# First loads over two queues, two transposes in a row, and z read back from DRAM, in a gated linear-attention kernel

## The chip, the cores and the metric

The kernel runs on one core of one Trainium2 chip. The metric is the device time of one execution in microseconds (us), the median of several runs. Beside it stands one execution that the hardware profiler recorded; all single durations below are from that one.

## What is computed

The function is a mixture of two blocks over the same x (2048 x 640, bf16), g * A(x) + (1 - g) * B, with its gradients to all inputs but B_x. A is linear attention with 32 heads of 20 columns, B a dense layer with ReLU. What matters here is the start of A, where keys are summed to z:

```
g = sigmoid((x * gate_w).sum(-1))
qkv = x @ wqkv                      # q, k, v: 32 heads of 20
pq, pk = phi(q), phi(k)             # phi(t) = t + 1 where t > 0, else exp(t), + 1e-6
kv  = einsum("bhsd,bhse->bhde", pk, v)
z   = einsum("bhsd->bhd", pk)       # sum of pk over the 2048 rows: 640 numbers
num = einsum("bhqd,bhde->bhqe", pq, kv)
den = einsum("bhqd,bhd->bhq", pq, z) + 1e-6
a   = (num / den) @ wo
b   = relu(x @ w1) @ w2
out = g * a + (1 - g) * b           # and the gradients of out
```

## The kernel before

x is cut into 16 chunks of 128 rows. The program goes through these stages, each a loop over chunks or over the five blocks of 128 columns:

1. First loads (lines 408 to 432). x chunks 0 to 4 come in as they are (`x_load`, L402, through `load_N`, L334); the other chunks are also loaded transposed by DMA (`load_T`, L325). wk is loaded in five blocks (`wk_load`, L405). SyncE (SP) and ScalarE (ACT) each issue DMAs from a queue of their own; instructions on one engine keep their order, and a DMA that has to wait holds what its engine has behind it.
2. The k phase (L477 to L507). `warm_up` (L459) runs matmuls on zeros. `xt(i)` (L437) transposes chunk i on TensorE (PE) and copies the result out of PSUM (L451, L452, or L347 by `copy_out`); chunks 3 and 4 share one PSUM tile of two banks, named xtp2 in the code and xtp_194 in the profile. `k_part(i, ks)` (L463) multiplies chunk i with blocks ks of wk; the tile is kp. After the last block come an exponential on ACT and two operations of VectorE (DVE), L396 and L397, which give pk. The PE order of chunks 0 to 4 is written out by hand (L478 to L502). The gate weights are transposed into an extra column of wk (L483, L484), so that k_part gives the gate too. The DMA transposes start after k_part(1, [2]) (L494).
3. `q_main(0)` and `q_main(1)` (L518), then the Y phase (L626 to L635): for each of five blocks m, Y = pk^T x over all chunks, with a column of ones behind x, so that column 640 of the PSUM tile yp is z for the block. ACT copies Y0 (L630), DVE the z column into `zc_t` (L633), 128 partitions by 5; DVE makes a diagonal block of it in `zd` (L634); SP transposes Y0 by DMA (L635).
4. z to all partitions (L637 to L639): ones times zd on PE gives z in every row (zp), ACT copies it to `zb`.
5. `h_half(i, half)` (L560): x @ w1, half a chunk's row; ReLU by ACT (L569, L572) or DVE (L574). `blockdiag` (L374): 50 small matmuls into bd, ACT copy (L385), ten DVE masks (L388), which give KVT. `q_den(i)` (L526) multiplies pq by zb on GpSimd (POOL, L528); `q_post(i)` (L530) reduces that on DVE (L534), takes the reciprocal, scales on POOL (L542) and transposes by DMA. `mt_tile(t)` (L647) needs KVT. `out_chunk(i)` (L587) needs the transposed h, the transposed pq and M.
6. The loop over pairs of chunks (from L671), and then the gradients, up to the last stage, which ends near 636 us.

The order of instructions on each engine is made by the framework's scheduler from the program's order and from its estimate of what is ready; only PE's order in stage 2 is fixed. PSUM tiles of tag PP share four buffers. The large SBUF buffers lie in one arena; the planner (`_Arena.plan`, L31) looks for an arrangement by seeded random reordering of the list of entries, with start and end times written by hand (L121 to L188), `zd` among them (L136).

The last gradient is stored near the end, from 128 partitions with five numbers each:

```
gcol = cpool.tile([P, KD], BF16, name="gcol")                          # L297
nc.scalar.dma_start(out_6.rearrange("(k p) -> p k", p=P), gcol[:])     # L1021
```

Of the kernel before, what the change touches and what calls it, by code (L numbers as in the profile page):

```python
# [8 lines left out]
ALU = mybir.AluOpType  # L9
AX = mybir.AxisListType  # L10
FP32 = mybir.dt.float32
BF16 = mybir.dt.bfloat16
PSUM = bass.MemoryType.PSUM

P = 128
# [66 lines left out]
def kernel(  # L82
# [5 lines left out]
    nc = tc.nc  # L88
    x2 = A_x.rearrange("b s d -> (b s) d")
# [3 lines left out]
    S, D = x2.shape  # L93
    F = B_w1.shape[1]
    NT = S // P
    KD = D // P
# [16 lines left out]
    ar = _Arena()  # L113
    B2 = 2
# [6 lines left out]
    T_Y, T_FF, T_DW2, T_X, T_FB, T_DW1, T_DWK, T_DX, T_END = 26, 48, 190, 273, 296, 432, 512, 556, 640  # L121
# [11 lines left out]
    ar.add("w1", KD * F * B2, 8, T_H)  # L133
    ar.add("w2", KF * D * B2, 12, T_DW2 + 10)
    ar.add("pk", NT * D * B2, 0, T_FF)
    ar.add("zd", D * B2, 0, T_FF - 5)  # L136
    ar.add("YT0", KD * D * B2, T_Y, T_FF + 5)
    ar.add("dzs", D * B2, T_X, T_FB + 50)
    ar.add("warm", 512 * B2, 0, 10)
# [55 lines left out]
    def aview(name, n_elems, **dims):  # L195
        o = ar.off(name) // 2
        v = arena[:, o:o + n_elems]
        if dims:
            (k, n), = dims.items()
            v = v.rearrange(f"p ({k} z) -> p {k} z", **{k: n})  # L200
        return v
# [7 lines left out]
    def mat(name):  # L209
        return aview(name, KD * D, k=KD)  # L210

    xN = aview("xN", NT * DQX, i=NT)
# [13 lines left out]
    xSg = [aview(f"xS{g}", G * D, k=KD) for g in range(NG)]  # L226
    doTg = [aview(f"doT{g}", G * D, k=KD) for g in range(NG)]
    hsg = [aview(f"hs{g}", G * FPAD, i=G) for g in range(NG)]
    zd, YT0_s = aview("zd", D), mat("YT0")
    dzs = aview("dzs", D)  # L230
    wk_s, wq_s, wv_s, wo_s = aview("wk", KD * DQX, k=KD), mat("wq"), mat("wv"), mat("wo")
    w1_s = aview("w1", KD * F, k=KD)
# [30 lines left out]

    dram = ctx.enter_context(tc.tile_pool(name="dram", bufs=1, space=bass.MemoryType.DRAM))
    pk_d = dram.tile([S, D], BF16, name="pk_d")
    pqg_d = dram.tile([S, D], BF16, name="pqg_d")
    KVT_d = dram.tile([D, D], BF16, name="KVT_d")
    e_d = dram.tile([S, D], BF16, name="e_d")
# [8 lines left out]
    cpool = ctx.enter_context(tc.tile_pool(name="const", bufs=1))  # L277
    tsb = ctx.enter_context(tc.tile_pool(name="ts", bufs=2))
    psp = ctx.enter_context(tc.tile_pool(name="ps", bufs=1, space=PSUM))
    ident = cpool.tile([P, P], BF16, name="ident")  # L280
# [2 lines left out]
                            pattern=[[-1, P]], channel_multiplier=1)  # L283
    gwb = cpool.tile([P, D], BF16, name="gwb")
    ones_sq = cpool.tile([P, P], BF16, name="ones_sq")
    zc_t = cpool.tile([P, KD], FP32, name="zc_t")
    MDw = cpool.tile([P, KD, BWID], BF16, name="MDw")
    zb = cpool.tile([P, D], BF16, name="zb")
    dzb = cpool.tile([P, D], BF16, name="dzb")
# [12 lines left out]
    def _nm(pfx):  # L302
        _cnt[0] += 1
        return f"{pfx}{_cnt[0]}"

    def pp(name="pp"):
        return psp.tile([P, 2, 512], FP32, tag="PP", bufs=4, name=_nm(name))
# [4 lines left out]
    def csl(i):  # L312
        return slice(i * P, (i + 1) * P)

    def flat(ps_tile):
        return ps_tile.rearrange("p b c -> p (b c)")
# [10 lines left out]
    def after(late, early, wait=False):  # L327

        tc.add_manual_dep(late.ins, early.ins.name, mybir.DependencyInfo(
            mybir.DependencyClass.Sync if wait else mybir.DependencyClass.NoSync,  # L330
            mybir.DependencyReason.DATA), reason="order of loads")

    def load_N(dst, src):
        return nc.sync.dma_start(dst, src.rearrange("(i p) d -> p i d", p=P))  # L334
# [4 lines left out]
    def mm_cols(ps_tile, lhsT, rhs_fn, start, stop, spl=DSPL, **kw):  # L339
        for b, (a, e) in enumerate(spl):  # L340
            mm = nc.tensor.matmul(ps_tile[:, b, 0:e - a], lhsT=lhsT, rhs=rhs_fn(a, e), start=start, stop=stop, **kw)  # L341
        return mm

    def copy_out(n, dst, src):
        if n % 2 == 0:
            return nc.scalar.copy(dst, src)
        return nc.vector.tensor_copy(dst, src)  # L347
# [44 lines left out]
    def phi_chain(ps_flat, dst):  # L392
        eb = tmp("tb", 8)
        nc.scalar.activation(eb[:], ps_flat, ACT.Exp)
        cp = tmp("tb", 8)
        nc.vector.tensor_scalar(cp[:], eb[:], 1.0, 1e-6, ALU.min, ALU.add)  # L396
        nc.vector.scalar_tensor_tensor(dst, ps_flat, 1.0 + 1e-6, cp[:], ALU.add, ALU.max)  # L397
# [1 line left out]

    warm = aview("warm", 512)  # L400
    nc.vector.memset(warm, 0.0)
    def x_load(a, b):  # L402
        return load_N(xN[:, a:b, 0:D], x2[a * P:b * P, :])

    def wk_load(eng, k):  # L405
        eng.dma_start(wk_s[:, k, 0:D], A_wqkv[k * P:(k + 1) * P, D:2 * D])

    nc.scalar.dma_start(gst[:], gate_w.rearrange("(k p) -> k p", p=P))
    x_load(0, 1)
    wk_load(nc.scalar, 0)  # L410
    x_load(1, 2)
    wk_load(nc.scalar, 1)
    x_load(2, 3)
    wk_load(nc.scalar, 2)
    wk_load(nc.sync, 3)
    wk_load(nc.sync, 4)
    for i in range(3, NPE):
        x_load(i, i + 1)
# [18 lines left out]
    def xt(i):  # L437
        if i < 3:
            tp = flat(pp("xtp"))[:, 0:D].rearrange("p (k s) -> p k s", k=KD)
        else:  # L440
            if i == 3:
                kps["x"] = psp.tile([P, 2, 1024], BF16, tag="PP", bufs=4, name="xtp2")
            tp = kps["x"][:, i - 3, 0:D].rearrange("p (k s) -> p k s", k=KD)
        for k in range(KD):
            if i < 3:
                nc.tensor.matmul(tp[:, k, :], lhsT=xN[:, i, csl(k)], rhs=ident[:], start=True, stop=True,
                                 skip_group_check=True)
            else:
                nc.tensor.transpose(tp[:, k, :], xN[:, i, csl(k)], ident[:])
        if i in (1, 2):  # L450
            nc.vector.tensor_copy(xTv[i][0][:, 0:2, :], tp[:, 0:2, :])  # L451
            nc.scalar.copy(xTv[i][0][:, 2:KD, :], tp[:, 2:KD, :])  # L452
        else:
            copy_out(0 if i == 4 else 1, xTv[i][0], tp)

    def xT(i, k):
        return xTv[i][0][:, k, xTv[i][1]]

    def warm_up(n, cols=512):  # L459
        for _ in range(n):  # L460
            nc.tensor.matmul(wp_[:, 0, 0:cols], lhsT=warm[:, 0:P], rhs=warm[:, 0:cols], start=True, stop=True)

    def k_part(i, ks):  # L463
        if 0 in ks:
            kps[i] = pp("kp")
        kp, last = kps[i], 3 if i < 3 else KD - 1
        for k in ks:
            mm = mm_cols(kp, xT(i, k), lambda a, e: wk_s[:, k, a:e], k == 0, k == last, spl=DSP1)
        if last in ks:
            nc.scalar.activation(rg_t[:, i:i + 1], flat(kp)[:, D:D + 1], ACT.Exp, scale=-1.0)  # L470
            phi_chain(flat(kp)[:, 0:D], pkN[:, i, :])
            if i % 4 == 3:
                nc.sync.dma_start(pk_d[(i - 3) * P:(i + 1) * P, :].rearrange("(i p) d -> p i d", p=P),
                                  pkN[:, i - 3:i + 1, :])
        return mm

    wp_ = pp("warm")  # L477
    with tc.manual_schedule(engines={mybir.EngineType.PE}):  # L478
        warm_up(4)
        warm_up(1, 256)  # L480
        xt(0)
        tp = psp.tile([P, KD, P], BF16, tag="PP", bufs=4, name="gwtp")
        nc.tensor.transpose(tp[:, 0, 0:KD], gst[:], ident[0:KD, 0:KD])  # L483
        nc.vector.tensor_copy(wk_s[:, :, D:D + 1], tp[:, 0, 0:KD].unsqueeze(2))  # L484
        warm_up(3)
        k_part(0, [0])
        xt(1)
        xt(2)
        k_part(1, [0])
        k_part(0, [1])  # L490
        k_part(1, [1])
        k_part(2, [0, 1])
        k_part(0, [2])
        after(xT_ld[0], k_part(1, [2]), wait=True)  # L494
        k_part(2, [2])
        k_part(0, [4, 3])
        xt(3)
        k_part(1, [4, 3])
        xt(4)
        k_part(2, [4, 3])  # L500
        k_part(3, range(KD))
        k_part(4, range(KD))  # L502
# [112 lines left out]
    def masks(early):  # L615
        after(nc.gpsimd.memset(KVT_s, 0.0), early, wait=True)  # L616
        after(nc.gpsimd.memset(MDw[:], 1.0), early, wait=True)
        for r in range(2 * KD):
            rel, md = HP * r - BW[r], MDw[r % 2 * HP:r % 2 * HP + HP, r // 2, :]
            nc.gpsimd.affine_select(out=md, in_=md, compare_op=ALU.is_ge, fill=0.0,  # L620
                                    base=rel, pattern=[[-DH, BWID // DH], [0, DH]], channel_multiplier=1)
            nc.gpsimd.affine_select(out=md, in_=md, compare_op=ALU.is_ge, fill=0.0,
                                    base=DH - 1 - rel, pattern=[[DH, BWID // DH], [0, DH]], channel_multiplier=-1)


    for m in range(KD):  # L626
        yp = pp("yp")
        for i in range(NT):
            mm_cols(yp, pkN[:, i, csl(m)], lambda a, e: xN[:, i, a:e], i == 0, i == NT - 1, spl=DSP1)
        yt = nc.scalar.copy(YT0_s[:, m, :], flat(yp)[:, 0:D])  # L630
        if m == 0:
            masks(yt)
        nc.vector.tensor_copy(zc_t[:, m:m + 1], flat(yp)[:, D:D + 1])  # L633
        nc.vector.tensor_scalar(zd[:, csl(m)], ident[:], zc_t[:, m:m + 1], None, ALU.mult)  # L634
        Y_ld = load_T(Y_s[:, :, csl(m)], YT0_s[:, m, :])  # L635
    h_half(0, 0)
    zp = pp("zp")  # L637
    mm_cols(zp, ones_sq[:], lambda a, e: zd[:, a:e], True, True)
    nc.scalar.copy(zb[:], flat(zp)[:, 0:D])  # L639
    q_den(0)  # L640
    h_half(0, 1)
    h_half(1, 0)
# [438 lines left out]
```

## Time and profile before

| | us |
|---|---|
| median of 3 runs | 637.62 |
| lowest and highest run | 637.07, 637.72 |
| the profiled execution | 637.72 |
| its span, first to last instruction | 636.0 |
| PE busy in the span | 631.1 |
| Y phase, first to last matmul | 32.4 to 54.4 |

The page's section 5 lists the costliest groups of instructions: line, engine, operation, what it writes and reads, count, busy us, mean ns, and idle us of the engine just before with what ended it. Section 6 lists the DMA issues with size and median us from issue to landing. Some names are those of the program: arena is the large SBUF buffer, so many different operands have this one name, and the line tells them apart. A bracket in a timeline line gives the idle time before it and what ended that.

### The profile page before, as it was taken

The page shows a single profiled execution, that of the slowest core. Times are in us where ns is not written, and L with a number is a line of the kernel's source. Part 1 is how long each engine was busy: PE and PEld are TensorE (multiplying, and loading weights), DVE is VectorE, ACT ScalarE, POOL GpSimd, SP SyncE. Part 2 cuts the span into 40 slices and gives each one's busy share as a digit, 9 for nine tenths or more (in the row PEclk, how much of TensorE's full clock was granted, in tenths as well). Part 3 has the DMA queues.
Part 4 walks back from the last instruction along what each step waited for, and adds up shares of the span by engine and source line. Part 5 has one row for each costly group of instructions (what it writes and reads, how often), then busy time and mean ns, then how long its engine had stood idle before and what let it go on. Part 6 is the DMA issues. An engine that isn't in the chain of part 4 may idle for free.

```text
span 636.0 us, 10575 instructions
## 1 busy us (share of the span) xinstructions
PE 631.1 (99%) x4482; PEld 351.9 (55%) x4482; DVE 270.1 (42%) x523; ACT 147.7 (23%) x208; POOL 97.7 (15%) x95
## 2 busy tenths in 40 slices
PE   8999999999999999999999999999999999999998
PEld 4555555555555555555555555555555555555554
DVE  4842864454444145555994241510016340004442
ACT  4513321122221123222153343331210011110000
POOL 0050742453334022322001000000000000000000
PEclk9999999999999999999999999999999999999999
DMA  6999996554454793942799998965147659991111
GB/s 177 309 395 210 195 247 148 121 92 88 124 120 97 192 197 103 213 134 73 166 187 215 258 262 183 224 151 126 49 117 180 170 111 231 238 262 42 42 42 43
DMA packets 228473, 103.93 MB, mean 163 GB/s; under 512 B 185098, under 2 KB 227722, under 8 KB 228426
## 3 DMA queue, kind: packets, MB, share of 16 engines
q1 hardware_dynamic: 217344, 90.48, 61.4%
q10 hardware_dynamic: 11082, 12.79, 6.0%
q8 instruction: 35, 0.57, 0.4%
q14 instruction: 12, 0.10, 0.0%
HBM read 28.43 MB, written 28.84 MB: 90 GB/s over the span
## 4 chain that ended last, share of the span: by engine, by line
PE 98%; ACT 1%; DVE 0%; issue 0%
PE w1p_5164 L917 1%; PE w1p_4741 L917 1%; PE w1p_4639 L917 1%; PE w1p_5289 L917 1%; PE w1p_5232 L917 1%; PE w1p_5096 L917 1%; PE w1p_5027 L917 1%; PE w1p_4873 L917 1%; PE w1p_4804 L917 1%; PE w1p_4571 L917 1%; PE op_2287 L341 1%; PE op_2250 L341 1%; PE op_2150 L341 1%; PE op_1956 L341 1%; PE op_1761 L341 1%; PE op_1567 L341 1%
## 5 line engine op out<-in xcount | busy, mean ns | idle before, releaser
L341 PEld LDWEIGHTS <-arena 128*128 128x128 bf16 x2978 | 230.4, 98 | 179.8 <-issue 2.1
L917 PEld LDWEIGHTS <-arena 128*128 128x128 bf16 x320 | 30.9, 98 | 26.6
L818 PEld LDWEIGHTS <-arena 128*128 128x128 bf16 x320 | 30.7, 98 | 26.2 <-issue 0.5
L565 PEld LDWEIGHTS <-arena 128*128 128x128 bf16 x320 | 30.0, 98 | 26.7 <-issue 1.8
L901 DVE TENSOR_TENSOR tb_4851<-dkp_4840,dzb 128x640 bf16<-128x640 f32 x1 | 0.8, 825 | 37.8 <-PE dkp_4840 L341 37.8
L1014 PEld LDWEIGHTS <-arena 128*128 128x128 bf16 x80 | 7.8, 98 | 9.5
L1019 DVE CAST gcol<-wqp_5514 128x1 bf16<-128x1 f32 x1 | 0.2, 161 | 28.0 <-ACT arena L1018 28.0
L616 POOL MEMSET arena<- 128x3200 bf16 x1 | 2.8, 2765 | 36.3 <-ACT arena L630 36.3
L1015 PEld LDWEIGHTS <-arena 128*128 128x128 bf16 x80 | 7.8, 98 | 0.0
L866 POOL MEMSET arena<- 128x3200 bf16 x1 | 2.8, 2764 | 32.8 <-PE dwo_3624 L367 32.8
L367 PEld LDWEIGHTS <-arena 128*128 128x128 bf16 x120 | 6.9, 97 | 1.4
L575 DVE COPY arena<-arena 128x64 bf16<-128x64 bf16 x16 | 6.1, 382 | 0.5
L917 PE MATMUL w1p_4571<-arena 128*128 128x432 bf16 x32 | 6.0, 346 | 0.0
L917 PE MATMUL w1p_4639<-arena 128*128 128x432 bf16 x32 | 6.0, 346 | 0.0
L917 PE MATMUL w1p_4741<-arena 128*128 128x432 bf16 x32 | 6.0, 346 | 0.0
L917 PE MATMUL w1p_4873<-arena 128*128 128x432 bf16 x32 | 6.0, 346 | 0.0
L917 PE MATMUL w1p_5096<-arena 128*128 128x432 bf16 x32 | 6.0, 346 | 0.0
L917 PE MATMUL w1p_5164<-arena 128*128 128x432 bf16 x32 | 6.0, 346 | 0.0
L917 PE MATMUL w1p_4804<-arena 128*128 128x432 bf16 x32 | 6.0, 346 | 0.0
L917 PE MATMUL w1p_5027<-arena 128*128 128x432 bf16 x32 | 6.0, 346 | 0.0
L917 PE MATMUL w1p_5232<-arena 128*128 128x432 bf16 x32 | 6.0, 346 | 0.0
L917 PE MATMUL w1p_5289<-arena 128*128 128x432 bf16 x32 | 6.0, 346 | 0.0
(1039 smaller groups left out, 1179.0 us busy)
## 6 DMA issues: line engine op xcount, KB each, us to landing
out_dram<-arena ACTq DMA_DIRECT2D x28, 160.0 KB, 3.8
arena<-in_A_x_dram SPq DMA_DIRECT2D x6, 640.0 KB, 5.1
pk_d<-arena SPq DMA_DIRECT2D x4, 640.0 KB, 9.6
arena<-in_grad_out_dram SPq DMA_DIRECT2D x4, 640.0 KB, 4.9
e_d<-arena SPq DMA_DIRECT2D x8, 320.0 KB, 2.8
out_dram<-arena ACTq DMA_DIRECT2D x8, 320.0 KB, 2.3
arena<-e_d SPq DMA_DIRECT2D x8, 320.0 KB, 4.3
dq_d<-arena SPq DMA_DIRECT2D x8, 320.0 KB, 3.8
```

What stands on the lines that cost most here:

```text
L341: mm = nc.tensor.matmul(ps_tile[:, b, 0:e - a], lhsT=lhsT, rhs=rhs_fn(a, e), start=start, stop=stop, **kw)
L367: nc.tensor.matmul(ps_tile[:, bank, a - HD * bank:e - HD * bank], lhsT=lhsT_fn(j), rhs=rhs_mat[:, j, a:e], start=bank not in seen, stop=LA ...
L565: nc.tensor.matmul(hp[:, nb, 0:NBW], lhsT=xT(i, k), rhs=w1_s[:, k, blk * NBW:(blk + 1) * NBW], start=(k == 0), stop=(k == KD - 1))
L575: nc.vector.tensor_copy(hs(i)[:, F:FPAD], hs(i)[:, F - FT:F])
L616: after(nc.gpsimd.memset(KVT_s, 0.0), early, wait=True)
L818: nc.tensor.matmul(gp[:, nb, 0:NBW], lhsT=doTg[i // G][:, k, gsl(i)], rhs=w2T_s[:, k, blk * NBW:(blk + 1) * NBW], start=(k == 0), stop=(k ...
L866: nc.gpsimd.memset(dKVT_s, 0.0)
L901: nc.vector.tensor_tensor(a_[:], flat(kp)[:, 0:D], dzb[:], ALU.add)
L917: nc.tensor.matmul(wp[:, nb, 0:NBW], lhsT=xN2[:, i, csl(m)], rhs=hs(i)[:, blk * NBW:(blk + 1) * NBW], start=(i == 0), stop=(i == NT - 1))
L1014: nc.tensor.matmul(wp[:, 0, :], lhsT=lhsT, rhs=dqN[:, i, 0:512], start=(i == 0), stop=(i == NT - 1))
L1015: nc.tensor.matmul(wp[:, 1, 0:D + 1 - 512], lhsT=lhsT, rhs=dqN[:, i, 512:D + 1], start=(i == 0), stop=(i == NT - 1))
L1019: nc.vector.tensor_copy(gcol[:, m:m + 1], flat(wp)[:, D:D + 1])
```

## The change

- The first loads: x chunk 0, wk blocks 0, 1, 2 and 4 and x chunks 3 and 4 are issued by SP; the gate weights, x chunks 1 and 2 and wk block 3 by ACT. Before, SP had x chunks 0, 1, 2, wk blocks 3, 4 and x chunks 3, 4; ACT had the gate weights and wk blocks 0, 1, 2.
- Three warm-up matmuls of 512 columns before the first k_part become one of 512 and one of 256.
- xt(4) stands directly behind xt(3), ahead of k_part(1, [4, 3]).
- zd and its arena entry, the five DVE products, the two matmuls into zp and the ACT copy to zb are gone. zc_t is bf16. ACT issues two DMAs in their place: zc_t to a DRAM tile of 640 numbers, and from there to all 128 partitions of zb.

```diff
-    ar.add("zd", D * B2, 0, T_FF - 5)
...
+    z_d = dram.tile([D], BF16, name="z_d")
...
-    zc_t = cpool.tile([P, KD], FP32, name="zc_t")
+    zc_t = cpool.tile([P, KD], BF16, name="zc_t")
...
-    def x_load(a, b):
-        return load_N(xN[:, a:b, 0:D], x2[a * P:b * P, :])
+    def x_load(a, b, eng=nc.sync):
+        return eng.dma_start(xN[:, a:b, 0:D], x2[a * P:b * P, :].rearrange("(i p) d -> p i d", p=P))
...
     nc.scalar.dma_start(gst[:], gate_w.rearrange("(k p) -> k p", p=P))
     x_load(0, 1)
-    wk_load(nc.scalar, 0)
-    x_load(1, 2)
-    wk_load(nc.scalar, 1)
-    x_load(2, 3)
-    wk_load(nc.scalar, 2)
-    wk_load(nc.sync, 3)
+    wk_load(nc.sync, 0)
+    x_load(1, 2, nc.scalar)
+    wk_load(nc.sync, 1)
+    x_load(2, 3, nc.scalar)
+    wk_load(nc.sync, 2)
+    wk_load(nc.scalar, 3)
     wk_load(nc.sync, 4)
...
-        warm_up(3)
+        warm_up(1)
+        warm_up(1, 256)
         k_part(0, [0])
...
         xt(3)
+        xt(4)
         k_part(1, [4, 3])
-        xt(4)
         k_part(2, [4, 3])
...
         nc.vector.tensor_copy(zc_t[:, m:m + 1], flat(yp)[:, D:D + 1])
-        nc.vector.tensor_scalar(zd[:, csl(m)], ident[:], zc_t[:, m:m + 1], None, ALU.mult)
         Y_ld = load_T(Y_s[:, :, csl(m)], YT0_s[:, m, :])
     h_half(0, 0)
-    zp = pp("zp")
-    mm_cols(zp, ones_sq[:], lambda a, e: zd[:, a:e], True, True)
-    nc.scalar.copy(zb[:], flat(zp)[:, 0:D])
+    nc.scalar.dma_start(z_d.rearrange("(k p) -> p k", p=P), zc_t[:])
+    nc.scalar.dma_start(zb[:], z_d.rearrange("(o d) -> o d", o=1).to_broadcast([P, D]))
     q_den(0)
```

## The prediction, made before the changed kernel was run

> **What bounds the kernel now.** I read the page first: busy time and the chain of work that ended last.
>
> ```profile
> PE 631.1 (99%) x4482; PEld 351.9 (55%) x4482; DVE 270.1 (42%) x523; ACT 147.7 (23%) x208; POOL 97.7 (15%) x95
> ...
> PE 98%; ACT 1%; DVE 0%; issue 0%
> ```
>
> TensorE (PE) runs without a break, so a saving counts only if PE gets shorter, and any wait that reaches PE is paid in full. Next I read the waits of the stretch 0 to 75 us, for PE alone.
>
> ```profile
> PE warm_126 L461 <- DVE arena L401: 1.3, 1, 1.3
> PE kp_227 L341 <- DVE arena L397: 0.2, 1, 0.2
> PE kp_166 L341 <- DVE arena L451: 0.2, 1, 0.2
> ```
>
> None is a wait for a load. Then the timeline (start, duration, engine, line, operation), at the start and where z is made:
>
> ```profile
> 4.67 0.17 DVE L484 COPY arena<-gwtp 128x5 bf16<-128x5 bf16 x1
> ...
> 5.19 0.74 PE L341 MATMUL kp_147<-arena 128*128 128x512 bf16 x2
> ...
> 10.20 0.49 DVE L347 COPY arena<-xtp_194 128x640 bf16<-128x640 bf16 x1 [2.94 <-PE xtp_194 L449]
> ...
> 10.75 0.44 PE L449 MATMUL xtp_194<-ident,arena 128*128 128x128 bf16 x5
> ```
> ```profile
> 56.03 0.43 PE L341 MATMUL zp_710<-arena,ones_sq 128*128 128x512 bf16 x2
> ...
> 61.23 0.49 ACT L385 CAST tb_793<-bd_742 128x400 bf16<-128x400 f32 x1
> ...
> 61.82 2.23 DVE L388 TENSOR_TENSOR arena<-tb_793,MDw 64x80 bf16<-64x80 bf16 x10 [2.16 <-ACT tb_793 L385]
> ...
> 64.26 0.48 PE L367 MATMUL mtp_845<-arena 128*128 128x140 bf16 x6
> ```
>
> In the first, PE's k_part(0) starts 0.35 us after the gate column was copied, and the second transpose of the shared tile right after DVE's copy. In the second, a chain without slack runs beside PE: ScalarE (ACT) copies bd (L385), VectorE (DVE) masks it (L388, done at 64.05), and PE's mt_tile(0) starts 0.21 later.
>
> The change stores z from 128 partitions, element by element, into DRAM. The kernel has exactly one DMA of that form already, the last gradient (gcol to out_6, L1021, the same 128 x 5 bf16 and the same pattern). I read its issue, the store just before it on ACT's queue, and the row of the stores behind it (L1050):
>
> ```profile
> out_dram<-gcol ACTq DMA_DIRECT2D x1, 1.2 KB, 15.4
> ```
> ```profile
> out_dram<-arena ACTq DMA_DIRECT2D x1, 160.0 KB, 12.2
> ```
> ```profile
> DMA to landing us min/median/max: 2.3/2.3/8.8
> ```
>
> 1.2 KB take 15.4 us to land; the 160 KB beside it take 12.2, though the median of that line is 4.8; and the first of seven 320 KB stores after it takes 8.8 where the median is 2.3. All three end at 581 to 586 us, although DMA moves next to nothing from 571.5 on. Today nobody waits for them.
>
> **What the Trainium skill says.** "DMA: Bandwidth & Descriptors", section "Issuing engines are not separate DMA queues": transfers from both queues run on the same 16 engines, and a second queue only saves issue time. The trace agrees: x and wk loads land 2.3 to 4.1 us after issue on either queue. Same page, "Rules for kernel authors": a last dimension that isn't contiguous becomes one descriptor per element, and a DMA that reads what another wrote has to wait for that one's semaphore on the issuing engine; its specifications add that below 512 B the engine reads, modifies and writes. The trace fits: 640 elements in 15.4 us, 24 ns each. Same page, "Queues, rings and completion order": a completion count lands only after every earlier write of that DMA engine, across its queues; the 12.2 and 8.8 us agree. "TensorE: Matmul & The Clock Gate", "Part 1: The HAM clock gate": half clock until a window of about 3.4 us was busy, and again after one idle window. The trace shows the first half: 128-column matmuls start 0.107 us apart until 6.26 us and 0.056 after. It has no idle window after that.
>
> **The change, part by part.** Times are on the clock of the profiled execution.
>
> *Loads.* Eleven loads of the same sizes stay; x1, x2, wk3 swap queues with wk0, wk1, wk2, place for place. By the old landings of those places: wk0 4.2, x1 4.4, wk1 5.4, x2 5.6, wk2 5.9, wk3 6.4 us. None is needed before 4.9, 5.5, 7.0, 6.0, 8.1 and 9.2. Worth 0; the cover is PE's earlier work, thinnest for x2 (0.4 us).
>
> *Warm-ups.* 1.5 matmuls of 0.427 us go. The first k_part needs the gate column copied at 4.84 (L484), so it starts near 4.92 instead of 5.19: **-0.27**.
>
> *x transposes side by side.* xt(4) today starts 0.06 us after DVE has copied xt(3) out of the same PSUM tile (10.69), though its data were there at 7.6: it waits for that copy. Today k_part(1) fills the time. Put directly behind xt(3) it waits with PE idle: 1.03 from xt(3) to xt(4), then 0.27, then two k_parts of 0.545 make 2.39 us until k_part(3). Today these are 2.24 (9.72 to 11.96), with 0.4 lost before k_part(3) for a PSUM buffer. **+0.15**. If xt(4) turns out not to wait, it is -0.45 instead.
>
> *zd and zp.* Five DVE products of 0.25 us go, where DVE waited 3.9 each time: 0. Two PE matmuls (0.27 from 56.03 to hp_716 at 56.30) and a 0.68 ACT copy go: -0.27 if PE is never stopped later, 0 if it is. A one-column zc_t in bf16 costs what it did.
>
> *z through DRAM.* Two DMAs are added on ACT's queue. The store is issued when the last zc_t is there: 55.29 + 0.06 - 0.12 (the sum so far) = 55.23. I take the twin's 15.4 us: it lands at **70.63**. From below the bound is about 2.5 us (a plain ACT store: 2.3); from above I allow 18 under the heavier traffic here.
>
> The read-back must wait for that, in ACT's order, and ACT does nothing meanwhile. It stands in the program before relu of h_half(1,0) and the bd copy. So ACT holds from 57.1 to 70.63, issues (0.45) at 71.08, then relu 0.98 to 72.06, bd copy 0.1 + 0.49 to 72.65, DVE masks 0.1 + 2.23 to 74.98, mt_tile(0) at 75.19. It was 64.26: **+10.9**, with the gains above already in it. PE runs dry meanwhile: its four PSUM buffers and KVT stop it at about 64. All the early gains except 0.12 are swallowed.
>
> *Cold PE.* Eleven idle us are far more than a window. PE restarts at half clock and loses half of that stretch: 3.4 us by the skill's page, 5.0 by this trace's start (1.26 to 6.26), so 1.7 to 2.5. I take **+2.0**.
>
> *zb itself.* The read-back is 160 KB; the row of one on ACT's queue says 2.8 us, the same broadcast for gwb 6.0 (behind others). It lands at 73.4 to 76.6, q_den(0) on POOL takes 0.14 + 1.39, so 75.0 to 78.2. DVE reaches the reduction of q_post(0) after the masks, at 75.0: between 0 and 3.2 us late, and everything behind it on DVE (phi of q_main(2), mt copies) with it. I take 0, because ACT's ring is empty.
>
> Other DMAs in the held time (the last Y transpose, YT_d, gwb, do, hT(0)) complete behind the store. If the Y transpose does, blockdiag's own matmuls start at 70.7: cold 2.0, copy 0.7, masks 2.3, mt_tile at 75.95, with hp_814 and qp_828 between; that comes to 12.3 to 13.1 in all, the same place.
>
> Sum: 10.9 + 2.0 = 12.9. The profiled execution took 637.72 (span 636.0 and 1.7 around it), the median of the runs is 637.62: **650.5**.
>
> **Rivals.** *A, the forecast* (0.72): ACT or the transposes wait for the store, 646.5 to 655. *B, not slower* (0.12): the store lands as an ordinary ACT store does. For this: the last of gcol's packets is done at 571.71 in the DMA records, 2.5 us after issue. Against it: the completion counts, three of them. It decides at one point: landing before 59.9 (4.7 us after issue) leaves relu and bd copy on time, zb comes by 64 and all is hidden; then -0.27 + 0.15 - 0.27 = -0.39, 637.2. Past that point each us costs one. *C, only q_post waits* (0.10): the built order puts the read-back behind ACT's and DVE's work, so that PE runs on to out_chunk(0), which needs pqT(0) at 76.5. zb 74.1, q_den 75.6, reduction to reciprocal 1.4, POOL 1.27, transpose 1.2 + 2.6: 82.1, so 5.6 late, and 2.0 cold: 645. *D, worse* (0.06): heavy traffic stretches the store to 18 us and zb is late too, or the arena, dealt anew because an entry is gone, holds back a load: over 655.
>
> **How the numbers follow.** A, C and D are slower (0.88). B splits: 0.2% (1.3 us) is about what a measurement of this kernel can tell from no change, and even with every gain and no wait (-1.0) B stays inside it: same 0.10, faster 0.02 for what I overlook. Range: A's ends are the neighbour's 12.2 us instead of 15.4 (647.3), no cold loss (648.5), zb 3.2 late (653.7) and a store of 18 us (653.1); down to C at 645 and up to 655.5 leaves B and most of D out, 0.18.
>
> **What would show it.** After the change: the z store 13 to 18 us to landing; ACT idle 11 us or more before L569 or L385; PE's first wait of more than 0.5 us near 60 to 76; 0.107 us steps of matmuls after it; xt(4) right behind the DVE copy with some 0.75 us of idle PE before it; the k phase starting 0.27 earlier. A z store under 5 us would make the forecast wrong at its main step.

## The result, and the profile after

The changed kernel takes 661.32 us (median of 6 runs, 658.33 to 663.19), the kernel before 637.31 beside it: ratio 1.0373, 95% interval 1.0342 to 1.0403. It is slower, and the store of z is behind most of it, as the prediction said, but by 24.0 us and not by 12.9. The profiled execution took 663.19, its span is 661.5 (before: 636.0). The six runs lie in two groups, 658.3 to 659.8 and 662.8 to 663.2, and the profiled one is the slowest of the upper group.

The page first: busy time, and the chain that ended last by engine and by line.

```profile
PE 631.7 (95%) x4403; PEld 353.6 (53%) x4479; DVE 264.5 (40%) x518; ACT 147.2 (22%) x207; POOL 98.0 (15%) x95
...
PE 86%; DMA 6%; DVE 5%; issue 1%; ACT 1%; POOL 0%; ACTq 0%; DVEq 0%; POOLq 0%
DMA z_d<-zc_t 3%; DVE f_3224 L796 2%; DMA zb<-z_d 1%; DMA f_3210<-f_3209 1%; PE w1p_5225 L916 1%; PE w1p_5020 L916 1%; PE w1p_4866 L916 1%; PE w1p_4797 L916 1%; PE w1p_5282 L916 1%; PE w1p_5157 L916 1%; PE w1p_5089 L916 1%; PE w1p_4734 L916 1%; PE w1p_4632 L916 1%; PE w1p_4564 L916 1%; PE op_2280 L341 1%
```

PE has as many busy us as before, but it is no longer the whole chain: two DMAs of z, a third DMA (f_3210, line 772) and a DVE chain (f_3224) hold it. The waits of PE say where, with total us, times and longest:

```profile
PE bd_735 L381 <- DMA arena<-arena: 14.3, 1, 14.3
PE mtp_874 L367 <- DVE arena L347: 3.4, 1, 3.4
PE dwo_3617 L367 <- DVE arena L347: 2.0, 1, 2.0
...
PE xtp_194 L449 <- DVE arena L347: 0.6, 1, 0.6
PE dp_4336 L341 <- ACT tb_4302 L821: 0.5, 1, 0.5
```

The first wait is for the last Y transpose, the second follows from the late zb, the third from the small copy f_3210. The DMA issues around them, with median us from issue to landing:

```profile
YT_d<-arena SPq DMA_DIRECT2D x1, 800.0 KB, 19.7
...
gwb<-in_gate_w_dram SPq DMA_DIRECT2D x1, 160.0 KB, 19.4
zb<-z_d ACTq DMA_DIRECT2D x1, 160.0 KB, 8.6
f_3210<-f_3209 ACTq DMA_DIRECT2D x1, 160.0 KB, 6.7
...
z_d<-zc_t ACTq DMA_DIRECT2D x1, 1.2 KB, 19.3
```

In the kernel before, two of these were:

```profile
YT_d<-arena SPq DMA_DIRECT2D x1, 800.0 KB, 4.5
...
gwb<-in_gate_w_dram SPq DMA_DIRECT2D x1, 160.0 KB, 6.0
```

The store of 1.2 KB takes 19.3 us, and the two that SP issued 1.1 and 1.7 us after it land 1.4 and 1.8 us after it. The timeline of that stretch (start, duration, engine, line, operation, idle time before it and what ended that):

```profile
54.54 0.16 DVE L634 CAST zc_t<-yp_657 128x1 bf16<-128x1 f32 x1 [4.20 <-ACT arena L631]
54.73 0.42 ACTq L637 DMA_DIRECT2D z_d<-zc_t  x1
...
59.18 0.76 PE L381 MATMUL bd_735<-arena 128*64 128x80 bf16 x31
74.05 0.34 ACTq L638 DMA_DIRECT2D zb<-z_d  x1
74.23 0.82 PE L381 MATMUL bd_735<-arena 128*64 128x80 bf16 x19 [14.29 <-DMA arena<-arena]
...
74.99 3.78 PE L566 MATMUL hp_807<-arena 128*128 128x432 bf16 x10
...
80.50 0.48 PE L367 MATMUL mtp_838<-arena 128*128 128x140 bf16 x6
...
82.80 1.39 POOL L529 TENSOR_TENSOR f_707<-tb_468,zb 128x640 f32<-128x640 bf16 x1 [36.28 <-DMA zb<-z_d]
...
84.23 0.82 DVE L535 TENSOR_REDUCE grd_798<-f_707 128x32 f32<-128x640 f32 x1 [6.03 <-POOL f_707 L529]
...
86.86 0.76 PE L367 MATMUL mtp_874<-arena 128*128 128x140 bf16 x6 [3.43 <-DVE arena L347]
```

PE stops in the middle of bd: 31 of its 50 matmuls run, the other 19 need the last Y transpose. SP had issued that one at 54.53, 0.2 us ahead of the store, but PE is released only 0.2 us after the store landed (54.73 + 19.3 = 74.03). PE comes back cold, at half clock (the granted clock is 0.50 from 74.2 to 78.6): ten hp matmuls take 3.78 us where warm ones, at full clock, take 1.99. Then zb, read back late, stops DVE for 6.03 us and through it PE a second time.

How late PE is against before (its shift), at the first matmul of a tile (after minus before): -0.86 at hp_709, +13.92 at hp_807, +16.24 at mtp_838, +19.83 at mtp_874, +21.11 at qp_931 (90.88 us), then nearly constant for 260 us, +21.39 at gp_3583 (354.16), +23.55 at dwo_3617, +24.95 at dp_3660 and +25.30 at dp_4336. So in this execution 21 us are lost around z, and some 4 more far from anything that the change touched.

### The profile page after: what moved, and what is told of

Read it like the earlier page. It is cut to its first block, busy times and chain, and to the rows that moved or that the text cites. A ratio compares the mean times of both kernels' runs of the same rounds, so it can differ in the third digit from the quotient of the medians.

```text
span 661.5 us, 10495 instructions
## 1 busy us (share of the span) xinstructions
PE 631.7 (95%) x4403; PEld 353.6 (53%) x4479; DVE 264.5 (40%) x518; ACT 147.2 (22%) x207; POOL 98.0 (15%) x95
## 4 chain that ended last, share of the span: by engine, by line
PE 86%; DMA 6%; DVE 5%; issue 1%; ACT 1%; POOL 0%; ACTq 0%; DVEq 0%; POOLq 0%
DMA z_d<-zc_t 3%; DVE f_3224 L796 2%; DMA zb<-z_d 1%; DMA f_3210<-f_3209 1%; PE w1p_5225 L916 1%; PE w1p_5020 L916 1%; PE w1p_4866 L916 1%; PE w1p_4797 L916 1%; PE w1p_5282 L916 1%; PE w1p_5157 L916 1%; PE w1p_5089 L916 1%; PE w1p_4734 L916 1%; PE w1p_4632 L916 1%; PE w1p_4564 L916 1%; PE op_2280 L341 1%
## 5 line engine op out<-in xcount | busy, mean ns | idle before, releaser
L381 PE MATMUL bd_735<-arena 128*64 128x80 bf16 x50 | 1.6, 226 | 14.3 <-DMA arena<-arena 14.3
L381 PEld LDWEIGHTS <-arena 128*64 128x64 bf16 x100 | 2.3, 120 | 15.0 <-issue 15.0
L388 DVE TENSOR_TENSOR arena<-tb_786,MDw 64x80 bf16<-64x80 bf16 x10 | 1.9, 195 | 17.4 <-ACT tb_786 L385 17.1
L529 POOL TENSOR_TENSOR f_707<-tb_468,zb 128x640 f32<-128x640 bf16 x1 | 1.4, 1392 | 36.3 <-DMA zb<-z_d 36.3
L916 PE MATMUL w1p_4797<-arena 128*128 128x432 bf16 x32 | 6.0, 346 | 0.0
L916 PE MATMUL w1p_4866<-arena 128*128 128x432 bf16 x32 | 6.0, 346 | 0.0
L916 PE MATMUL w1p_5020<-arena 128*128 128x432 bf16 x32 | 6.0, 346 | 0.0
L916 PE MATMUL w1p_5157<-arena 128*128 128x432 bf16 x32 | 6.0, 346 | 0.0
L916 PE MATMUL w1p_5225<-arena 128*128 128x432 bf16 x32 | 6.0, 346 | 0.0
L916 PE MATMUL w1p_5282<-arena 128*128 128x432 bf16 x32 | 6.0, 346 | 0.0
```

The costliest lines, as they stand in the source:

```text
L381: nc.tensor.matmul(ps[h_ * HP:(h_ + 1) * HP, 0, m * BWID:(m + 1) * BWID], lhsT=lhsT_mat[:, k, r * HP:(r + 1) * HP], rhs=rhs_mat[:, k, BW[r ...
L916: nc.tensor.matmul(wp[:, nb, 0:NBW], lhsT=xN2[:, i, csl(m)], rhs=hs(i)[:, blk * NBW:(blk + 1) * NBW], start=(i == 0), stop=(i == NT - 1))
```

## Experiments

**Theory**, after the result: the element-wise store of z is slow in itself, it holds the completion of other DMAs, and PE stops for the Y transpose; the read-back, late by the same time, costs a second stop; the last 4 us come from the arena, dealt anew without zd. **Rivals**: it is ACT's wait in its own order that hurts; or any round trip through DRAM is too slow here; or the early part (loads, warm-ups, xt) has a share; or the last 4 us are a late echo of the shift.

### e1, e2: which part of the change

e1 is the changed kernel with z as before, e2 the kernel before with the z part alone:

```diff
# e1, against the changed kernel
+    ar.add("zd", D * B2, 0, T_FF - 5)
...
-    nc.scalar.dma_start(z_d.rearrange("(k p) -> p k", p=P), zc_t[:])
-    nc.scalar.dma_start(zb[:], z_d.rearrange("(o d) -> o d", o=1).to_broadcast([P, D]))
+    zp = pp("zp")
+    mm_cols(zp, ones_sq[:], lambda a, e: zd[:, a:e], True, True)
+    nc.scalar.copy(zb[:], flat(zp)[:, 0:D])
```

> The loads in order of use, the warm-ups and xt(4) beside xt(3) stay as changed; z goes through the PE again and zd has its place in the arena. Theory (all of the loss is in z): 636.7 to 637.4 us, 0 to 0.6 under the kernel before. Rival (the xt part's 0.58 us wait and the swapped loads cost something that comes back later): over 638.

> The kernel before with nothing but the z part of the change. Theory (all of the loss is in z, zd's place in the arena included): 660 to 663 us, 23 to 25 over the kernel before, with a wait of 13 to 15 us for the Y transpose on PE. Rival (the early part takes a share, or it shifts the z store into a busier moment): under 655.

e1: 637.75 us, ratio 1.0002 (0.9992 to 1.0011). e2: 660.20 us, ratio 1.0353 (1.0333 to 1.0373), with 11.8 us of wait for the Y transpose, less than the 13 to 15 expected. e1 lies between its two expectations, but can't be told from the kernel before. So the loss is in z, the place of zd in the arena included.

### e3, e9, e10: the last 4 us

e3 keeps the arena's zd entry, unused; e9 is e1 with zd outside the arena; e10 is e9 with the w1 transposes ordered behind the copy w2o<-w2e.

```diff
# e3, against the changed kernel
+    ar.add("zd", D * B2, 0, T_FF - 5)
# e9, against e1
-    ar.add("zd", D * B2, 0, T_FF - 5)
...
+    zd = cpool.tile([P, D], BF16, name="zd")
# e10, against e9 (the third w1 transpose likewise)
-        load_T(w1T_s[:, 0:KF - 1, q_ * 320:(q_ + 1) * 320], B_w1[q_ * 320:(q_ + 1) * 320, 0:(KF - 1) * P])
+        after(load_T(w1T_s[:, 0:KF - 1, q_ * 320:(q_ + 1) * 320], B_w1[q_ * 320:(q_ + 1) * 320, 0:(KF - 1) * P]), w2o_ld)
```

> The changed kernel, with the entry of zd left in the arena though nobody uses it, so that every buffer lies where it lay before. Theory (of the 24 us about 4 come from the buffers dealt anew, which lets the w1 transposes pass the small copy w2o<-w2e on the way): 657 us, and that copy lands in 2.5 to 3.5 us instead of 6.7. Rival (the 4 us are a late consequence of the shift at the store): 661 as before.

> e1 with zd moved out of the arena into a buffer of its own: z goes through the PE, nothing is stored, but the buffers lie as in the changed kernel and SP's queue has the changed kernel's order (the first two w1 transposes one dq store earlier, ahead of the copy w2o<-w2e). Theory (this order alone is worth the late part): 640 to 642 us, the small copy lands in 5 to 7 us, and the wait on PE behind the dz chain is there. Rival (the late part needs the shift at the z store, too): 637 to 638.

> e9 with the w1 transposes put behind the small copy w2o<-w2e again by a dependency of order; the buffers lie as in e9. Theory (the copy was overtaken in the transfers): the copy lands in 2.5 to 3.5 us, 637 to 638. Rival (where the buffers lie costs it, not the order on SP): 640 to 642 as e9.

e3: 656.53 us, ratio 1.0302 (1.0283 to 1.0321); PE's shift is +17.7 ahead of dwo and behind it: the last 4 us are gone. e9: 639.85, ratio 1.0041 (1.0027 to 1.0055). e10: 638.13, ratio 1.0011 (1.0004 to 1.0018). Each lies 0.1 to 0.2 us outside the range of its theory and over 1.8 us from its rival's. The small copy's landing in the issues of before, of e9 and of e10:

```profile
f_3217<-f_3216 ACTq DMA_DIRECT2D x1, 160.0 KB, 2.8
```
```profile
f<-f ACTq DMA_DIRECT2D x1, 160.0 KB, 6.4
```
```profile
f<-f ACTq DMA_DIRECT2D x1, 160.0 KB, 3.5
```

The timeline of the changed kernel shows the way from there to PE:

```profile
313.52 9.35 SPq L325 DMA_TRANSPOSE arena<-in_B_w_dram  x2
319.55 0.53 ACTq L772 DMA_DIRECT2D f_3210<-f_3209  x1
326.43 1.53 POOL L773 TENSOR_TENSOR arena<-f_3209,f_3210 64x640 bf16<-64x640 f32 x1 [8.24 <-DMA f_3210<-f_3209]
327.99 0.82 DVE L794 TENSOR_TENSOR f_3260<-arena,u_all 128x640 f32<-128x640 bf16 x1 [7.26 <-POOL arena L773]
...
358.77 0.48 PE L367 MATMUL dwo_3617<-arena 128*128 128x140 bf16 x6 [2.00 <-DVE arena L347]
359.08 3.27 PE L817 MATMUL gp_3625<-arena 128*128 128x432 bf16 x10
```

With the buffers elsewhere, the scheduler puts the two w1 transposes ahead of a dq store in SP's order, and they start before the copy (in the kernel before at 302.31, after the copy at 298.45). The copy comes behind them, its fp32 buffers come free late, and DVE's chain of dz operations (lines 794 to 798), which runs almost without a break, starts 3.9 us later against PE. PE meets it at dwo: 2.0 us, then 1.7 at a lower clock (3.27 and 2.43 instead of 1.99 twice), then 0.5. e9 has the same 2.0 and 0.5 without the clock loss. The rival of an echo falls with e9, that of the place alone with e10.

### e4, e5: the store, or the round trip

e4 transposes zc_t on PE, so that the store writes five rows of 256 bytes; e5 is e1 with the element-wise store added and no reader.

```diff
# e4, against the changed kernel
+    nc.tensor.transpose(zt[0:KD, 0, :], zc_t[:], ident[:])
+    nc.vector.tensor_copy(zr[:], zt[0:KD, 0, :])
-    nc.scalar.dma_start(z_d.rearrange("(k p) -> p k", p=P), zc_t[:])
+    nc.scalar.dma_start(z_d.rearrange("(k p) -> k p", p=P), zr[:])
# e5, against e1 (zc_b is a bf16 copy of zc_t)
+    nc.scalar.dma_start(z_d.rearrange("(k p) -> p k", p=P), zc_b[:])
```

> The changed kernel, with zc_t transposed on the PE to five rows of 128 before its store, so that the store writes five pieces of 256 bytes instead of 640 of 2 bytes; read-back and place are unchanged. Theory (the element-wise store is what is slow, and it holds the Y transpose): the store lands in 2 to 3 us, the 14.3 us wait on PE goes, the 4 us of the arena stay: 640 to 643 us. Rival (a round trip through DRAM with a broadcast read-back is too slow at this place, whatever its form): over 650.

> The kernel of e1 (z through the PE, zd in the arena, nothing reads z_d) with the changed kernel's element-wise store of z added at the same place; its result is used by nobody, and ACT waits for nothing. Theory (the store in flight holds the Y transpose and so stops PE, with no reader needed): the store lands in 15 to 19 us, PE waits 11 to 14 us for the Y transpose, 650 to 654 us. Rival (what hurt was ACT waiting for the store and the late zb): 637 to 640.

e4: 640.44 us, ratio 1.0047 (1.0033 to 1.006). The read-back is issued 1.20 us after the store's issue (55.83 and 57.03; the store's own landing isn't on record) and lands in 5.6, the wait for the Y transpose is gone, and the 2.0 us at dwo stay. So a round trip as such isn't what is slow. e5: 651.85, ratio 1.0225 (1.0207 to 1.0242). Its waits on PE:

```profile
PE bd L383 <- DMA arena<-arena: 11.7, 1, 11.7
```

Nobody reads z_d, and ACT has no DMA to wait for; PE stops all the same, so ACT's wait isn't needed. e5 minus e1 is 14.1 us: 11.7 of waiting and the cold clock (ten hp matmuls take 3.78 us here, too).

The packets show how the others are held. These are the DMA totals from 57.7 to 72 us, first of e5, then of e6 (below), in which PE waits for no transpose:

```profile
DMA packets 542, 0.68 MB, mean 48 GB/s; under 512 B 8, under 2 KB 542, under 8 KB 542
```
```profile
DMA packets 6775, 3.46 MB, mean 242 GB/s; under 512 B 5077, under 2 KB 6773, under 8 KB 6773
```

In e5 all of the store's own packets are over by then, and so are those of the Y transpose (pieces of 256 bytes; only 8 packets are under 512): of the transpose only the completion is missing. But the transfers that come behind crawl as well: the 16 DMA engines are as busy as in e6 and move a fifth.

### e6, e7, e8, e11, e13, e14, e15: what makes the store slow

All are e5 with another z_d, which nobody reads: elements 512 bytes apart (e6); the first column alone (e7) or the last (e15), 128 elements; fp32 (e8); the five columns of 128 elements 4096, 1024 or 512 bytes apart (e11, e13, e14).

```diff
# e6
+    nc.scalar.dma_start(z_d[:, 0:1].rearrange("(k p) o -> p (k o)", p=P), zc_b[:])   # z_d [D, 256]
# e7, and e15 with zc_b[:, KD - 1:KD]
+    nc.scalar.dma_start(z_d[0:P].rearrange("(p o) -> p o", o=1), zc_b[:, 0:1])
# e8
+    nc.scalar.dma_start(z_d.rearrange("(k p) -> p k", p=P), zc_t[:])                 # z_d in fp32
# e11, e13, e14
+    nc.scalar.dma_start(z_d[:, 0:P].rearrange("k p -> p k"), zc_b[:])                # z_d [KD, 2048], 512, 256
```

> e5 with the 640 elements written 512 bytes apart in DRAM instead of side by side. If writes of two bytes to the same stretch of memory wait for each other: the store lands in 2 to 4 us and the time is 637 to 639. If each element has its price wherever it goes: like e5, 650 to 654.

> e5 with one column of zc instead of five: 128 elements of two bytes, and the rest of z_d is left unwritten. If the price is by the element (17 us for 640 is 27 ns each): landing in 4 to 6 us, at about 60, and little or no wait on PE, 637 to 639. If it is a fixed price of such a store: like e5, 650 to 654.

> e5 with z_d and the stored elements in fp32: 640 elements of 4 bytes. If it is the number of elements: like e5, 650 to 654. If pieces under 4 bytes are what is slow: the store lands in 2 to 6 us, 637 to 640.

> e5 (nobody reads z_d) with the five columns of 128 elements written 4096 bytes apart, each column still side by side: 256 bytes hold 128 elements as in e5, 512 bytes hold 128 instead of 256. If it is elements in the same 64 to 256 bytes that wait for each other: landing as in e5, 16 to 17 us, 650 to 653. If the stretch that counts is 512 bytes or more: as e8, landing in 10 to 12 us, 643 to 647.

> e11 with the columns 1024 bytes apart instead of 4096. Theory (writes of two bytes go one after the other, some 41 ns each by e11's 26.5 us after its last packet for 640, wherever their addresses fall to the same unit of memory; 4096 apart is the same unit, 1024 apart is not): 128 x 41 ns = 5.3 us after the last packet, landing 8 to 9 us after the issue, about 64; PE waits 3 to 5 us for the Y transpose, 640 to 643 us. Rival (separate blocks as such are slow, so that e11's spacing plays no part): as e11, 28 us to landing and 660 or more.

> e11 with the columns 512 bytes apart: the 2560 bytes that e8 covers with pieces of 4 bytes, half filled with pieces of 2. Theory (it is the spread over units of memory that counts, not the size of the piece): as e8, 10 to 12 us to landing, 643 to 647 us. Rival (pieces of 2 bytes are slower than pieces of 4): over 14 us to landing, 648 or more.

> e5 with the last column alone: 128 elements, which are there only when all five would be, so that the store starts at the same moment as in e5. Theory (one after the other in one unit of memory at 41 ns): 5.3 us after the last packet, landing 7 to 9 us after the issue, PE waits 2 to 5 us, 639 to 643. Rival (the price is mostly fixed, as e7's 15.0 us for 128 elements says): 13 to 16 us to landing, 648 or more.

The store's row in the issues of e5, e6, e15, e8, e14, e13 and e11, in this order (size, us to landing):

```profile
z_d<-zc_b ACTq DMA_DIRECT2D x1, 1.2 KB, 16.9
```
```profile
z_d<-zc_b ACTq DMA_DIRECT2D x1, 1.2 KB, 3.2
```
```profile
z_d<-zc_b ACTq DMA_DIRECT2D x1, 0.2 KB, 15.1
```
```profile
z_d<-zc_t ACTq DMA_DIRECT2D x1, 2.5 KB, 11.4
```
```profile
z_d<-zc_b ACTq DMA_DIRECT2D x1, 1.2 KB, 17.2
```
```profile
z_d<-zc_b ACTq DMA_DIRECT2D x1, 1.2 KB, 17.3
```
```profile
z_d<-zc_b ACTq DMA_DIRECT2D x1, 1.2 KB, 28.9
```

Times: e6 637.15 us, ratio 0.9998 (0.9989 to 1.0006); e8 646.03, 1.0142 (1.0111 to 1.0173); e11 663.56, 1.0404 (1.039 to 1.0419); e7 646.59, 1.0139 (1.0124 to 1.0155); one run each of e13 652.22, e14 655.17 and e15 650.44.

e6 is decisive. The same 640 pieces of two bytes, 512 bytes apart, land in 3.2 us, and nothing waits. So neither the number of pieces nor their size is the price by itself: it is where they go, many of them to the same stretch of memory. My figures for a price by the piece then failed one after the other. e7 should have landed in 4 to 6 us and took 15.0 (the scheduler also moved it up to 38.0 us, where all five Y transposes came late, 3.7 us of waits in all); e15, at the right moment, took 15.1, nearly as long as five times as many elements, as its rival said. My theory for e13 (one unit of memory after the other) gave 8 to 9 us, and it took 17.3: its rival, separate blocks being slow as such, fell with it, since e11 takes 28.9. e11 itself missed both of its expectations, e8 lay between its two, and e14's rival held.

What stands, e11 apart, is an order of the runs by their fullest stretch. 128 pieces in 256 bytes take 15 to 17 us, whether there is one such stretch, five side by side, or five that are 512 or 1024 bytes apart; 64 pieces of four bytes in 256 bytes take 11.4; one piece in 512 bytes takes 3.2. Whether e8 is faster for its fewer pieces in 256 bytes or for their size (e14's rival) no run separates. In e15 the last packet is done at 56.98 and the landing comes at 70.31, 13.3 us or 104 ns for each of the 128. How short that stretch is (no element-wise store here has fewer than 64 pieces in 256 bytes but e6), and why columns 4096 bytes apart take 28.9, stays open.

### e12: both mends, and e16: the changed kernel again

e12 is e4 with e3's arena entry; e16 is the changed kernel, unchanged.

> The changed kernel with the two mends that the runs point to: z stored as five rows (e4) and the place of zd kept in the arena (e3). If the element-wise store and the arena are the whole loss: 637.2 to 638.3 us, no more than 0.1% from the kernel before, and no wait on PE over 0.6 us. If something of the round trip is left: 639 or more.

> The changed kernel once more. If the store's 19.3 us belong to where its buffers lie: again 19 to 20 us to landing and 661 to 663 us. If it is the execution: 16 to 18 us and 657 to 660.

e12: 639.16 us, ratio 1.0035 (1.0022 to 1.0049): the second expectation holds, something of the round trip is left. Its two largest waits around z on PE are 0.5 and 0.3 us, both on DVE. The timeline of e12 shows why DVE is late:

```profile
61.70 3.32 DVE L389 TENSOR_TENSOR arena<-tb,MDw 64x80 bf16<-64x80 bf16 x10 [2.17 <-ACT tb L386]
...
63.56 1.40 POOL L530 TENSOR_TENSOR f<-tb,zb 128x640 f32<-128x640 bf16 x1 [16.55 <-DVE arena L389]
```

zb comes at 63.4 instead of 57.8, so q_den's product on POOL now lies beside DVE's ten masks (in the kernel before it ran at 57.93), and these take 3.32 us instead of 2.23. The Trainium skill, "Advanced Engine Details and Errata", "VectorE Performance Modes", says that DVE's second SBUF port is shared with GpSimd, so that GpSimd and DVE's modes with two ports block each other. This fits, but the trace doesn't show the mode of the masks, and no run here moved the product alone. e16, one run: 658.21 us, the store 16.6 us and the small copy 6.2, so the 19.3 us were that execution. PE's shift is 18.3 us ahead of dwo and 20.0 behind it: here the late part is 1.7 and not 4. No version tried beats the kernel before by more than the noise.

## Why the prediction was right or wrong

**Right.** The cause, its place and its direction: the store of z is slow, PE stops near 60 and comes back cold. The twin (gcol's store) was the right row to read, and rival B (the store lands as an ordinary one does) is what e4 and e6 make of it: with rows, or with spread elements and no reader, the store's loss is gone. The xt step is exact: from xt(3) at 9.00 to k_part(3) at 11.39 are 2.39 us, with the wait behind DVE's copy:

```profile
10.02 0.44 PE L449 MATMUL xtp_194<-ident,arena 128*128 128x128 bf16 x5 [0.58 <-DVE arena L347]
```

The cold clock was put at +2.0. At the pace of before, the 19 matmuls of bd left at 74.23 take 0.39 (1.02 for all 50), hp_807 1.83 and qp_821 1.36; that would be 77.81 for mtp_838, which starts at 80.50: 2.7.

**The path, right only in its second form.** The 10.9 us were worked out along ACT, which waits for the store and brings relu, the bd copy and the masks late. The alternative named in passing, that the last Y transpose completes behind the store, is what happened: PE stood still from 59.9 on, in bd, not from 64. In e5 ACT waits for no DMA, and 14.1 us are lost. Both paths start from the same landing, so the size came near though the path worked out was not the one that ended last.

**Mis-sized: the store.** Taken as 15.4 us, allowed up to 18, it was 19.3 in the profiled execution and 16.6 to 17.1 in e2, e3, e5 and e16. The store alone costs 14.1 us by e5, where the sum had 12.9 for the store and nothing else. The reason given, "24 ns each", is wrong though its total was near: e6 has the same 640 elements in 3.2 us.

**Failed: "I take 0, because ACT's ring is empty"** for zb. The read-back, 2.8 to 6.0 in the prediction, took 8.6, and 6.6 to 6.9 in e2, e3 and e16: it comes back together with what the store had held, YT_d, gwb, the do load and an hT transpose. That these share its delay is read from the trace; no run took them away. With nothing held it took 5.6 (e4), inside the prediction's range, and by the prediction's own sum 5.6 would have made DVE 2.8 us late: an empty ACT ring was no reason for 0. DVE was 6.03 us late and PE 3.43, plus 1.3 at a lower clock after it (the shift grows from 19.83 to 21.11; ten hp matmuls take 2.89 us). e3 minus e5 prices the reader at 4.7 us (656.53 and 651.85; 3.2 between their two profiled executions).

**Failed: the arena, left in rival D with 0.06.** Dealt anew, it held back no load but changed the order of SP's DMAs: 2.1 us by e9 minus e1, 1.7 in e16's trace, 3.7 by e2 minus e3, and 4.8 by the changed kernel minus e3 (661.32 and 656.53, not run side by side).

**Early part.** k_part(0) came at 4.82 (4.92 predicted), k_part(3) 0.57 us earlier than before where the sum had 0.12: in this execution the five 128-column matmuls behind k_part(0) run at full clock (0.44 us), before they took 0.74, which no part of the sum had. The loads' swap was put at 0; PE's waits for x chunks are 0 to 1.8 us from one execution to the next, 1.0 in e2 with the old order too. e1 leaves nothing to measure.

Sum by experiments: e1 0.0, the store 14.1, the reader 4.7, the arena 2.1: 20.9, where 24.0 was measured, and 20.4 in e16 (658.21 beside 637.81). An arena of 4.8 closes the sum only because e3 minus e1 is the store and the reader, so that the 4.8 are whatever is left. The 3.1 us that are missing lie in the spread of the changed kernel's own runs: the middle one of its lower group lost 22.1 us, that of the upper group 25.6. In the profiled one the store took 2.7 us longer than in e16, and PE lost 1.7 at a lower clock behind dwo. Why the runs differ so stays open. The predicted 12.9 answers to the store's 14.1; the reader and the arena are what it lacks.

## What to carry to other kernels

A DMA that scatters single elements side by side in DRAM can be dear not only for its own reader but for the DMAs around it; put the numbers into rows on an engine first (here one small transpose), or spread them. When a late transfer is released, price what returns with it, not the transfer alone. And a buffer taken out of a planned memory is a change to the order of DMAs elsewhere: keep the entry, or look at the queues far from the edit.

## What the runs showed of the hardware

- Pieces of two bytes are not slow by their size alone. The Trainium skill, "DMA: Bandwidth & Descriptors", "Specifications", says that below 512 bytes the engine reads, modifies and writes; e6's 640 pieces of two bytes are far below it and land in 3.2 us. Crowded, 128 to a stretch of 256 bytes, they take 15 to 17 us (16.6 to 19.3 with a reader), and 28.9 with the columns 4096 bytes apart.
- The store's own packets don't show it: in e5 the last packet of the store is done at 57.61, 2.4 us after the issue, and it lands at 72.09. The packets of the other DMAs do: from 57.7 to 72 us they move 48 GB/s, where e6 has 242.
- Ten DVE masks with a POOL product beside part of them take 3.32 us instead of 2.23 (e12, e4).
